# Two units ahead of the weights: reordering the start of an attention + SwiGLU kernel

## Chip, cores, metric

One core of a Trainium2 chip. The metric is device time in microseconds (us), median of several executions. A ratio in this text is the mean time of one kernel's fast runs over that of the other's fast runs of the same rounds, so it is not quite the ratio of the medians quoted beside it. In the profile's lines PE is TensorE, DVE is VectorE, ACT is ScalarE and POOL is GpSimd; square brackets give the idle time of the engine before a step and what ended it, by the profile. A profile covers one execution.

## The reference, cut

```python
B, H, S, D = 4, 8, 768, 48                # r, k, v; w, u per head and channel
for t in range(S):                        # attention with a decaying state
    cur = einsum('bhd,bhe->bhde', u * kt, vt)
    y[:, :, t] = einsum('bhd,bhde->bhe', rt, state + cur)
    state = w * state + einsum('bhd,bhe->bhde', kt, vt)
x = y.transpose(0, 2, 1, 3).reshape(3072, 384)
g = x @ w_gate                            # 384 x 1536
return (g * sigmoid(g) * (x @ w_val)) @ w_out   # 1536 x 384
```

Inputs are float64: r, k, v reach the chip as fp32, the three weights are rounded from float64 bits to fp32 inside the kernel.

## The kernel before

The sequence is cut into 24 units of 128 tokens. A unit goes through `scale` (GpSimd: khat, rhat), `turn` (TensorE transposes, ACT copies kT and rT), `diagonal` (the u term into At), `scores` (TensorE, then a masked copy on DVE), `outputs` (y, then ACT's xT) and `update` (u_ps, the state Z). Two units give a group of 12 gate/value pieces (`gv`), and later 6 projection parts (`o_ps`). Steps interleave them: step s turns unit s, scores unit s - 1, finishes unit s - 2, and in five gaps it rounds weight chunks ("R") and emits pieces ("F").

```python
def round_act():      # chunk n: magnitude and low part
    act.activation(mags[n], hi, AF.Abs, scale=2.0**-112)
    act.activation(lows[n], lo, AF.Copy, scale=2.0**-29)     # lows: two buffers
def round_dve():      # sign, then magnitude into the weight; frees the load buffer
    dve.tensor_scalar(dst, hi, -(1 << 31), None, ALU.bitwise_and)
    dve.scalar_tensor_tensor(dst, mag, 3, dst, ALU.logical_shift_left, ALU.bitwise_or)
    load_weights()
def round_pool():     # the rounding add
    pool.tensor_tensor(dst, dst, low, ALU.add)
def round_weights():  # one "R": GpSimd on chunk n, DVE on n + 1, ACT on n + 2
    if done["dve"] > done["pool"]: round_pool()
    if done["act"] > done["dve"]: round_dve()
    round_act()
def diagonal(i):
    if i < 6:
        for h in range(H): act.activation(At[i % 2][:, h, :], ident, AF.Identity, scale=du[:, h])
    else:
        pool.tensor_mul(At[i % 2], ident (broadcast), du (broadcast))
# ... cut
EARLY = [("R", "", "", "", "R"), ("R", "", "R", "", ""), ("R", "", "R", "", ""),
    ("R", "", "RF", "F", "F"), ("RF", "F", "RF", "F", "F"), ("RF", "F", "RF", "F", "RF"),
    ...]                               # the last line four times; later steps "F" only
```

A piece f of the first two groups is emitted only when its chunks (2 per pair of pieces) have had their add emitted; otherwise "F" does nothing.

Of the kernel before, what the change touches and what calls it, by code (L numbers as in the profile page):

```python
# [9 lines left out]
FP32 = mybir.dt.float32  # L10
INT32 = mybir.dt.int32
UINT32 = mybir.dt.uint32
AF = mybir.ActivationFunctionType
ALU = mybir.AluOpType
AX = mybir.AxisListType
P = 128
# [6 lines left out]
def fast(  # L23
# [25 lines left out]
    B, H, S, D = r.shape  # L49
    D2 = 2 * D  # L50
    VW = 2 * D + 16
    HP = H // 2
    NCH = S // P
    N = B * NCH
# [6 lines left out]
    ps_a = ctx.enter_context(tc.tile_pool(name="ps_a", bufs=5, space=bass.MemoryType.PSUM))  # L61
# [40 lines left out]
    def load_v(i):  # L102
        c, b = divmod(i, B)
        rows = slice(P * c, P * (c + 1))
        for e in range(2):
            sp.dma_start(
                out=v_ld[i % 4][:, :, 64 * e : 64 * e + D],
                in_=v[b, :, rows, :].rearrange("(a e) t d -> e t a d", e=2)[e],
            )
# [22 lines left out]
    def load_weights():  # L132
        n = next_chunk("load")
        if n is not None:
            src = chunks[n][0].bitcast(INT32)
            bits[n] = three.tile([P, WN, 2], INT32, name="w_bits", tag="w_bits")
            sp.dma_start(
                out=bits[n][:].rearrange("p (c f) two -> p c (f two)", c=src.shape[1]), in_=src
            )
# [5 lines left out]
    def round_act():  # L145
        n = next_chunk("act")
        if n is not None:
            lo, hi = bits[n][:, :, 0], bits[n][:, :, 1]
            mags[n] = two.tile([P, WN], INT32, name="w_mag", tag="w_mag")
            lows[n] = two.tile([P, WN], INT32, name="w_low", tag="w_low")  # L150
            act.activation(
                mags[n][:].bitcast(FP32), hi.bitcast(FP32), AF.Abs, scale=float(2.0**-112)
            )
            act.activation(lows[n][:], lo.bitcast(UINT32), AF.Copy, scale=float(2.0**-29))

    def round_dve():
        n = next_chunk("dve")
        if n is not None:
            dst = chunks[n][1].bitcast(INT32)
            c = dst.shape[1]  # L160
            hi = bits.pop(n)[:, :, 1].rearrange("p (c f) -> p c f", c=c)
            mag = mags.pop(n)[:].rearrange("p (c f) -> p c f", c=c)
# [4 lines that stand above are left out]
    def round_pool():  # L167
        n = next_chunk("pool")
        if n is not None:
            dst = chunks[n][1].bitcast(INT32)  # L170
            low = lows.pop(n)[:].rearrange("p (c f) -> p c f", c=dst.shape[1])
            pool.tensor_tensor(dst, dst, low, ALU.add)  # L172

    def round_weights():

        if done["dve"] > done["pool"]:
            round_pool()
        if done["act"] > done["dve"]:
            round_dve()
        round_act()  # L180
# [3 lines left out]
    def own_product(i):  # L184
        kl, rl = k_ld[i % 2], r_ld[i % 2]
        rk = two.tile([P, H, D], FP32, name="rk", tag="rk")
        pool.tensor_mul(rk[:], rl[:], kl[:])  # L187
        pool.tensor_mul(rk[:], rk[:], ub[:])  # L188
        du = three.tile([P, H], FP32, name="du", tag="du")
        dve.tensor_reduce(du[:], rk[:], axis=AX.X, op=ALU.add)  # L190
        dus[i] = du
# [9 lines left out]
        in_=bass.AP(tensor=u.tensor, offset=u.offset, ap=[[0, P], [1, H * D]]),  # L201
    )
    load(1)
    for n in range(3):
        load_weights()

    make_identity(nc, ident[:])

# [13 lines left out]
    for l in range(7):  # L222
        n = 1 << l
        f = sq[:, l, :].unsqueeze(2).to_broadcast([D2, HP, n])
        dve.tensor_mul(pw[:, :, P - 2 * n : P - n], pw[:, :, P - n : P], f)
    for n in (1, 0):
# [5 lines left out]
            act.copy(kscale[:].rearrange("p h d -> p (h d)"), x)  # L232
        else:
            dve.reciprocal(rscale[:].rearrange("p h d -> p (h d)"), x)
    dve.tensor_mul(
        wL[:], sq[:, 7, :].unsqueeze(2).unsqueeze(3).to_broadcast([D2, HP, 2, D]),
        own[:].unsqueeze(1).unsqueeze(3).to_broadcast([D2, HP, 2, D]),
    )

    pool.memset(mask[:], 1.0)  # L240
    pool.affine_select(
        out=mask[:], in_=mask[:], compare_op=ALU.is_gt, fill=0.0,
        base=0, pattern=[[1, P]], channel_multiplier=-1,
    )
    own_product(0)
    own_product(1)


    dve.tensor_tensor(bad[:], held[:], wcol[:], ALU.not_equal)
    dve.tensor_reduce(badc[:], bad[:], axis=AX.X, op=ALU.add)  # L250
    dve.memset(ones[:], 1.0)
    n_ps = ps_a.tile([P, HP, P], FP32, name="n_ps", tag="a")
    pe.matmul(n_ps[0:1, 0, 0:1], badc[:], ones[:], start=True, stop=True)
    act.copy(outside, n_ps[0:1, 0, 0:1])


    turned = {}

    def scale(i):
        pool.tensor_mul(khat[i % 4][:], k_ld[i % 2][:], kscale[:])  # L260
        pool.tensor_mul(rhat[i % 2][:], r_ld[i % 2][:], rscale[:])  # L261
        load_v(i)
        if i + 2 < N:
            load(i + 2)

    def diagonal(i):

        du = dus.pop(i)
        if i < 6:
            for h in range(H):  # L270
                act.activation(At[i % 2][:, h, :], ident[:], AF.Identity, scale=du[:, h : h + 1])
        else:
            pool.tensor_mul(  # L273
                At[i % 2][:], ident[:].unsqueeze(1).to_broadcast([P, H, P]),
                du[:].unsqueeze(2).to_broadcast([P, H, P]),
            )

    def pair(t, a):
        return t[:, 2 * a : 2 * a + 2, :].rearrange("p e d -> p (e d)")
# [1 line left out]
    def turn(i):  # L281
        for nm, t in (("kT", khat[i % 4]), ("rT", rhat[i % 2])):
            tp = ps_a.tile([P, HP, P], FP32, name="tp", tag="a")
            for a in range(HP):
                pe.transpose(tp[0:D2, a, :], pair(t, a), ident[:])  # L285
            if nm == "kT":
                for e in range(2):
                    act.activation(  # L288
                        kT[i % 2][:, :, e, :], tp[0:D2], AF.Identity, scale=own[:, e : e + 1]
                    )  # L290
            else:
                turned[i] = three.tile([D2, HP, P], FP32, name=nm, tag=nm)
                act.copy(turned[i][:], tp[0:D2])  # L293

    def scores(i, half):
        ps = ps_a.tile([P, HP, P], FP32, name="s_ps", tag="a")
        for n in range(4):
            a, e = divmod(4 * half + n, 2)
            pe.matmul(  # L299
                ps[:, n, :], kT[i % 2][:, a, e, :], turned[i][:, a, :],  # L300
                start=True, stop=True, skip_group_check=True,
            )
        dve.copy_predicated(  # L303
            At[i % 2][:, 4 * half : 4 * half + 4],
            mask[:].bitcast(INT32).unsqueeze(1).to_broadcast([P, HP, P]), ps[:],
        )
# [28 lines left out]
    def update(i):  # L335
# [17 lines left out]
        else:  # L353
            dve.tensor_add(z[:], ps[:], z[:])  # L354
            pool.tensor_mul(z[:], z[:], wL[:].rearrange("p a e d -> p a (e d)"))  # L355


    hT = {}

# [37 lines left out]
    def feed(n):  # L397
        for _ in range(n):
            ready = [k for k, (need, _) in enumerate(todo) if need <= done["pool"]]
            if ready:  # L400
                todo.pop(ready[0])[1]()

    def queue(g):
        parts = [(NW, lambda p=p: project(g - 1, p // 3, p % 3)) for p in range(6)] if g > 1 else []
        if g == 2:
            todo.extend((NW, lambda p=p: project(0, p // 3, p % 3)) for p in range(6))
        for f in range(FC):
            need = 2 * (f // 2) + 2 if g < 2 else NW
            todo.append((need, lambda f=f: gate_value(g, f)))
            if parts and 2 <= f < 8:  # L410
                todo.append(parts.pop(0))


    EARLY = [
        ("R", "", "", "", "R"),
        ("R", "", "R", "", ""),
        ("R", "", "R", "", ""),
        ("R", "", "RF", "F", "F"),
        ("RF", "F", "RF", "F", "F"),
        ("RF", "F", "RF", "F", "RF"),  # L420
        ("RF", "F", "RF", "F", "RF"),
        ("RF", "F", "RF", "F", "RF"),
        ("RF", "F", "RF", "F", "RF"),
    ]

    def gap(s, n):
        for what in EARLY[s][n] if s < len(EARLY) else ("F" * (3, 2, 2, 3, 2)[n]):
            if what == "R":
                round_weights()
            else:  # L430
                feed(1)

    round_weights()
    scale(0)
    for s in range(N + 2):
        if 1 <= s <= N:
            diagonal(s - 1)
        if s + 1 < N:
            if s > 0:
                own_product(s + 1)  # L440
            scale(s + 1)
        if s < N:
            turn(s)
        gap(s, 0)
        if 1 <= s <= N:
            scores(s - 1, 0)
            gap(s, 1)
            scores(s - 1, 1)
        gap(s, 2)
        if s >= 2:  # L450
            outputs(s - 2)
            if s % 2:
                queue((s - 3) // 2)
            gap(s, 3)
            update(s - 2)
        gap(s, 4)
    assert done["pool"] == NW
    feed(len(todo))
    for p in range(6):
# [414 lines left out]
```

## Time and profile before

| | kernel before |
|---|---|
| median | 737.14 us (736.28 to 738.16, 6 runs) |
| span in the profile | 736.8 us |
| TensorE busy | 696.1 us (94%) |
| first gate/value piece | 47.6 us |
| hole in TensorE | 115 to 124 us |

Two things take time here besides TensorE's own work: the first 47 us, and the hole. The lines that show both are in the prediction below. How to read them: where one engine is busy to the end, the time is its work plus what it failed to do early; so count the work done by a given moment, not the idle time of the others.

### The profile page before, as it was taken

To read this page: it belongs to the slowest core of one execution; us is meant where nothing else is said; L and a number is where in the kernel's file an instruction comes from. 1 tells how busy PE (TensorE), PEld (TensorE's weight loads), DVE (VectorE), ACT (ScalarE), POOL (GpSimd) and SP (SyncE) were. 2 spreads that over 40 slices of the span, in tenths; PEclk is the share of its full clock that TensorE was granted. 3 is DMA by queue.
4 is the path that set the end of the run, shared out by engine and by line. 5 is a ranking of instruction groups with operands and counts; after the bars stand their busy time and mean duration, and the time that the engine had idled before them with its cause. 6 is when DMAs were issued, how large, how long until landed. Compare 5 with 4: busy or idle time off the path is not lost.

```text
span 736.8 us, 10255 instructions
## 1 busy us (share of the span) xinstructions
PE 696.1 (94%) x4298; PEld 558.2 (76%) x4298; DVE 223.4 (30%) x443; ACT 165.1 (22%) x352; POOL 184.0 (25%) x159
## 2 busy tenths in 40 slices
PE   2669997999999999999999999999999999999997
PEld 2558886867788787787788787788788778777773
DVE  6755566302222132222132232222223212212120
ACT  2965652211111121111121122021111112011110
POOL 5974526430303030303033033032122211000000
PEclk9779998999999999999999999999999999999999
DMA  8974461120201010201021020111100000000000
GB/s 218 255 212 126 111 171 23 33 55 1 44 12 33 12 43 1 44 12 33 12 44 33 12 44 12 31 29 26 33 23 12 12 12 2 12 11 2 11 12 25
DMA packets 85768, 33.99 MB, mean 46 GB/s; under 512 B 76368, under 2 KB 79568, under 8 KB 85712
## 3 DMA queue, kind: packets, MB, share of 16 engines
q1 hardware_dynamic: 82256, 28.52, 16.5%
q10 hardware_dynamic: 3456, 4.72, 1.8%
q8 instruction: 36, 0.59, 0.3%
q14 instruction: 20, 0.16, 0.1%
HBM read 28.51 MB, written 4.72 MB: 45 GB/s over the span
## 4 chain that ended last, share of the span: by engine, by line
PE 88%; POOL 5%; issue 2%; DMA 1%; DVE 1%; ACT 1%; SPq 0%; POOLq 0%
PE gv L366 49%; PE o_ps L384 25%; PE y_ps L329 5%; PE s_ps L299 5%; PE tp L285 2%; PE u_ps L342 2%; DMA r_ld<-in_r_dram 1%; POOL rk L187 1%; POOL wo L172 1%; POOL wg L172 1%; POOL rhat L261 1%; POOL rk L188 1%; POOL khat L260 1%; ACT xT L333 1%; DVE wo L164 0%
## 5 line engine op out<-in xcount | busy, mean ns | idle before, releaser
L366 PE MATMUL gv<-xT,wg 128*128 128x256 f32 x864 | 215.5, 386 | 15.0 <-ACT xT L333 9.9
L366 PE MATMUL gv<-xT,wv 128*128 128x256 f32 x864 | 212.4, 382 | 0.0
L384 PE MATMUL o_ps<-wo,hT 128*128 128x384 f32 x576 | 197.0, 487 | 0.6 <-ACT o_sb L390 0.6
L366 PEld LDWEIGHTS gv<-xT,wg 128*128 128x128 f32 x864 | 159.8, 192 | 46.4 <-ACT xT L333 12.1
L373 DVE TENSOR_TENSOR sg<-sg,gv 128x256 f32<-128x256 f32 x144 | 60.5, 420 | 413.1 <-ACT sg L372 413.1
L366 PEld LDWEIGHTS gv<-xT,wv 128*128 128x128 f32 x864 | 165.9, 192 | 23.1
L384 PEld LDWEIGHTS o_ps<-wo,hT 128*128 128x128 f32 x576 | 107.8, 190 | 62.5 <-ACT o_sb L390 1.2
L372 ACT ACTIVATE sg<-gv 128x256 f32<-128x256 f32 x144 | 55.2, 384 | 402.9 <-PE gv L366 402.9
L355 POOL TENSOR_TENSOR Z<-Z,wL 96x384 f32<-96x384 f32 x16 | 16.1, 1008 | 359.4 <-DVE Z L354 359.4
L374 DVE TENSOR_TENSOR hT<-sg,gv 128x256 f32<-128x256 f32 x144 | 60.5, 420 | 4.9
L299 PEld LDWEIGHTS s_ps<-rT,kT 96*128 96x128 f32 x384 | 52.5, 204 | 6.3 <-ACT rT L293 0.3
L299 PE MATMUL s_ps<-rT,kT 96*128 96x128 f32 x384 | 52.8, 287 | 0.0
L303 DVE COPY_PREDICATED At<-mask,s_ps 128x512 f32<-128x512 int32 x48 | 34.3, 732 | 45.3 <-PE s_ps L299 45.3
L273 POOL TENSOR_TENSOR At<-ident,du 128x1024 f32<-128x1024 f32 x18 | 34.1, 1894 | 38.0 <-PE y_ps L329 38.0
L329 PE MATMUL y_ps<-At,v_ld 128*32 128x128 f32 x768 | 34.9, 273 | 0.0
L288 ACT ACTIVATE kT<-tp,own 96x512 f32<-96x512 f32 x48 | 30.1, 675 | 1.3 <-PE tp L285 0.5
L329 PE MATMUL y_ps<-rT,Z 96*32 96x128 f32 x480 | 30.2, 278 | 0.0
L329 PEld LDWEIGHTS y_ps<-At,v_ld 128*32 128x32 f32 x768 | 29.1, 109 | 0.9 <-issue 0.8
L187 POOL TENSOR_TENSOR rk<-r_ld,k_ld 128x384 f32<-128x384 f32 x24 | 27.6, 1148 | 4.3 <-DMA r_ld<-in_r_dram 4.3
L390 ACT COPY o_sb<-o_ps 128x384 f32<-128x384 f32 x24 | 11.5, 479 | 73.7 <-PE o_ps L384 73.7
L260 POOL TENSOR_TENSOR khat<-k_ld,kscale 128x384 f32<-128x384 f32 x24 | 24.0, 999 | 13.3 <-PE u_ps L342 13.3
L333 ACT COPY xT<-y_ps 128x384 f32<-128x384 f32 x24 | 11.5, 478 | 63.7 <-PE y_ps L329 63.7
(55 smaller groups left out, 341.2 us busy)
## 6 DMA issues: line engine op xcount, KB each, us to landing
k_ld<-in_k_dram SPq DMA_DIRECT2D x24, 192.0 KB, 2.8
r_ld<-in_r_dram SPq DMA_DIRECT2D x24, 192.0 KB, 3.3
w_bits<-in_moe_w_gate_dram SPq DMA_DIRECT2D x6, 768.0 KB, 6.9
w_bits<-in_moe_w_val_dram SPq DMA_DIRECT2D x6, 768.0 KB, 5.9
v_ld<-in_v_dram SPq DMA_DIRECT2D x48, 96.0 KB, 2.6
w_bits<-in_moe_w_out_dram SPq DMA_DIRECT2D x6, 768.0 KB, 4.4
out_dram<-o_sb ACTq DMA_DIRECT2D x24, 192.0 KB, 1.9
ub<-in_u_dram SPq DMA_DIRECT2D x1, 192.0 KB, 4.8
```

The costliest lines, as they stand in the source:

```text
L187: pool.tensor_mul(rk[:], rl[:], kl[:])
L260: pool.tensor_mul(khat[i % 4][:], k_ld[i % 2][:], kscale[:])
L273: pool.tensor_mul(At[i % 2][:], ident[:].unsqueeze(1).to_broadcast([P, H, P]), du[:].unsqueeze(2).to_broadcast([P, H, P]),)
L288: act.activation(kT[i % 2][:, :, e, :], tp[0:D2], AF.Identity, scale=own[:, e : e + 1])
L299: pe.matmul(ps[:, n, :], kT[i % 2][:, a, e, :], turned[i][:, a, :], start=True, stop=True, skip_group_check=True,)
L303: dve.copy_predicated(At[i % 2][:, 4 * half : 4 * half + 4], mask[:].bitcast(INT32).unsqueeze(1).to_broadcast([P, HP, P]), ps[:],)
L329: pe.matmul(ps[32 * q : 32 * q + 32, cc, :], *rows[q][n], start=(n == 0), stop=(n == len(rows[q]) - 1), skip_group_check=True,)
L366: pe.matmul(gv[:, o, :].rearrange("p (i t) -> p i t", i=2), wt[:, c, P * f : P * (f + 1)], xT[:, 2 * g % NX : 2 * g % NX + 2, c, :], start ...
L372: act.activation(sg[:], gv[:, 0, :], AF.Sigmoid)
L373: dve.tensor_mul(sg[:], sg[:], gv[:, 0, :])
L374: dve.tensor_mul(hT[g][:, f, :], sg[:], gv[:, 1, :])
L384: pe.matmul(ps[:], hT[g][:, f, P * j : P * (j + 1)], wo[:, f, :], start=(f == 0), stop=(f == FC - 1),)
```

## The change

The intent: get TensorE to its first pieces early, by sending units 0 and 1 through turn, scores and y back to back with only two of 18 weight chunks rounded, then give it six pieces a step in steps 6 to 9. In passing, the diagonals of the first six units go from ACT to GpSimd.

```diff
-    for n in range(3):
-        load_weights()
+    load_weights()
+    load_v(0)
+    load_weights()
+    load_v(1)
+    load_weights()
 # ... in diagonal(i):
-        if i < 6:
-            for h in range(H):
-                act.activation(At[i % 2][:, h, :], ident[:], AF.Identity, scale=du[:, h : h + 1])
-        else:
-            pool.tensor_mul(...)
+        pool.tensor_mul(...)
 # ... the count of decay values out of range moves from the start to step 12
+    EARLY = {3: ("RF", "F", "RF", "", "F"), 4: ("RF", "F", "RF", "F", "RF"),
+        5: ("RF", "F", "RF", "F", "RF"), 6: ("RF", "F", "RFF", "F", "RF"),
+        7, 8, 9: as 6}
+    scale(0); scale(1)
+    round_act(); round_act(); round_dve()
+    turn(0); turn(1)
+    diagonal(0); scores(0, 0); scores(0, 1); diagonal(1)
+    round_pool(); round_dve()
+    scores(1, 0); scores(1, 1)
+    round_pool(); own_product(2); scale(2); round_act()
+    outputs(0); outputs(1); queue(0)
+    own_product(3); scale(3)
+    # ... wL
+    turn(2); feed(1); update(0); round_weights(); feed(1); update(1)
-    for s in range(N + 2):
+    for s in range(3, N + 2):
```

More of the change, by code (lines that the diff above doesn't have):

```diff
@@ L234, in fast @@
             dve.reciprocal(rscale[:].rearrange("p h d -> p (h d)"), x)
-    dve.tensor_mul(
-        wL[:], sq[:, 7, :].unsqueeze(2).unsqueeze(3).to_broadcast([D2, HP, 2, D]),
-        own[:].unsqueeze(1).unsqueeze(3).to_broadcast([D2, HP, 2, D]),
-    )
+    own_product(0)
+    own_product(1)
     pool.memset(mask[:], 1.0)
@@ L244, in fast @@
     )
-    own_product(0)
-    own_product(1)
-    dve.tensor_tensor(bad[:], held[:], wcol[:], ALU.not_equal)
-    dve.tensor_reduce(badc[:], bad[:], axis=AX.X, op=ALU.add)
-    dve.memset(ones[:], 1.0)
-    n_ps = ps_a.tile([P, HP, P], FP32, name="n_ps", tag="a")
-    pe.matmul(n_ps[0:1, 0, 0:1], badc[:], ones[:], start=True, stop=True)
-    act.copy(outside, n_ps[0:1, 0, 0:1])
     turned = {}
@@ L261, in scale @@
         pool.tensor_mul(rhat[i % 2][:], r_ld[i % 2][:], rscale[:])
-        load_v(i)
+        if i >= 2:
+            load_v(i)
         if i + 2 < N:
@@ L268, in diagonal @@
         du = dus.pop(i)
-        if i < 6:
-            for h in range(H):
-                act.activation(At[i % 2][:, h, :], ident[:], AF.Identity, scale=du[:, h : h + 1])
-        else:
-            pool.tensor_mul(
-                At[i % 2][:], ident[:].unsqueeze(1).to_broadcast([P, H, P]),
-                du[:].unsqueeze(2).to_broadcast([P, H, P]),
-            )
+        pool.tensor_mul(
+            At[i % 2][:], ident[:].unsqueeze(1).to_broadcast([P, H, P]),
+            du[:].unsqueeze(2).to_broadcast([P, H, P]),
+        )
     def pair(t, a):
@@ L355, in update, with count_outside @@
             pool.tensor_mul(z[:], z[:], wL[:].rearrange("p a e d -> p a (e d)"))
+    def count_outside():
+        dve.tensor_tensor(bad[:], held[:], wcol[:], ALU.not_equal)
+        dve.tensor_reduce(badc[:], bad[:], axis=AX.X, op=ALU.add)
+        dve.memset(ones[:], 1.0)
+        n_ps = ps_a.tile([P, HP, P], FP32, name="n_ps", tag="a")
+        pe.matmul(n_ps[0:1, 0, 0:1], badc[:], ones[:], start=True, stop=True)
+        act.copy(outside, n_ps[0:1, 0, 0:1])
     hT = {}
@@ L411, in queue, with gaps @@
                 todo.append(parts.pop(0))
-    EARLY = [
-        ("R", "", "", "", "R"),
-        ("R", "", "R", "", ""),
-        ("R", "", "R", "", ""),
-        ("R", "", "RF", "F", "F"),
-        ("RF", "F", "RF", "F", "F"),
-        ("RF", "F", "RF", "F", "RF"),
-        ("RF", "F", "RF", "F", "RF"),
-        ("RF", "F", "RF", "F", "RF"),
-        ("RF", "F", "RF", "F", "RF"),
-    ]
-    def gap(s, n):
-        for what in EARLY[s][n] if s < len(EARLY) else ("F" * (3, 2, 2, 3, 2)[n]):
+    def gaps(s, n):
+        for what in EARLY[s][n] if s in EARLY else ("F" * (3, 2, 2, 3, 2)[n]):
             if what == "R":
@@ L431, in gap @@
                 feed(1)
+    EARLY = {
+        3: ("RF", "F", "RF", "", "F"),
+        4: ("RF", "F", "RF", "F", "RF"),
+        5: ("RF", "F", "RF", "F", "RF"),
+        6: ("RF", "F", "RFF", "F", "RF"),
+        7: ("RF", "F", "RFF", "F", "RF"),
+        8: ("RF", "F", "RFF", "F", "RF"),
+        9: ("RF", "F", "RFF", "F", "RF"),
+    }
+    scale(0)
+    scale(1)
+    round_act()
+    round_act()
+    round_dve()
+    turn(0)
+    turn(1)
+    diagonal(0)
+    scores(0, 0)
+    scores(0, 1)
+    diagonal(1)
+    round_pool()
+    round_dve()
+    scores(1, 0)
+    scores(1, 1)
+    round_pool()
+    own_product(2)
+    scale(2)
+    round_act()
+    outputs(0)
+    outputs(1)
+    queue(0)
+    own_product(3)
+    scale(3)
+    dve.tensor_mul(
+        wL[:], sq[:, 7, :].unsqueeze(2).unsqueeze(3).to_broadcast([D2, HP, 2, D]),
+        own[:].unsqueeze(1).unsqueeze(3).to_broadcast([D2, HP, 2, D]),
+    )
+    turn(2)
+    feed(1)
+    update(0)
     round_weights()
-    scale(0)
-    for s in range(N + 2):
-        if 1 <= s <= N:
+    feed(1)
+    update(1)
+    for s in range(3, N + 2):
+        if s <= N:
             diagonal(s - 1)
         if s + 1 < N:
-            if s > 0:
-                own_product(s + 1)
+            own_product(s + 1)
             scale(s + 1)
@@ L443, in fast @@
             turn(s)
-        gap(s, 0)
-        if 1 <= s <= N:
+        gaps(s, 0)
+        if s <= N:
             scores(s - 1, 0)
-            gap(s, 1)
+            gaps(s, 1)
             scores(s - 1, 1)
-        gap(s, 2)
-        if s >= 2:
+        gaps(s, 2)
+        if s >= 4:
             outputs(s - 2)
@@ L453, in fast @@
                 queue((s - 3) // 2)
-            gap(s, 3)
+            gaps(s, 3)
             update(s - 2)
-        gap(s, 4)
+        gaps(s, 4)
+        if s == 12:
+            count_outside()
     assert done["pool"] == NW
```

## The prediction

> **What bounds the kernel now.** I read the page's 40 slices first, then TensorE's waits, then the chain of waits, then the engines' timelines of the first 140 us.
>
> The slices say that TensorE (PE) is the bound from about 55 us on, and is not before that:
>
> ```profile
> PE   2669997999999999999999999999999999999997
> POOL 5974526430303030303033033032122211000000
> PEclk9779998999999999999999999999999999999999
> ```
>
> One slice is 18.4 us. The first three PE digits are 2, 6, 6, the seventh is 7, and all others are 9 but the last. The granted clock dips in the second, third and seventh slices. So there are two losses: the start, and a hole near 120 us. TensorE's waits before 130 us give them names (total, times, longest):
>
> ```profile
> PE t_ps L229 <- DVE pw L225: 7.9, 1, 7.9
> PE gv L366 <- ACT xT L333: 6.4, 2, 5.8
> PE n_ps L253 <- DVE ones L251: 5.5, 1, 5.5
> PE gv L366 <- DVE hT L374: 5.1, 2, 4.2
> PE u_ps L342 <- DVE At L303: 3.4, 1, 3.4
> ```
>
> After 130 us only 4.2 us of waits are left in 607 us. From there on the time is TensorE's work, so a gain can only come from having done more of it by some early moment. The chain of waits gives the price list of that work, and shows the hole (start, us, what):
>
> ```profile
> 44.43 1.82 POOL wg L172
> 46.28 0.91 ACT w_low L154
> 47.19 0.37 ACT xT L333
> 47.60 5.49 PE gv L366 x12
> ...
> 60.23 0.89 PE s_ps L299 x8
> 61.13 2.59 PE gv L366 x12
> ...
> 67.20 1.03 PE y_ps L329 x32
> ...
> 71.03 0.68 PE u_ps L342 x8
> ...
> 74.32 0.87 PE tp L285 x8
> ...
> 112.35 1.85 POOL At L273
> ...
> 119.19 2.48 POOL wo L172
> ```
>
> At full clock a gate/value piece (gv) costs 2.6, a turn of one unit (tp) 0.87, both halves of its scores 2 x 0.89 = 1.8, a first-chunk y 1.03, an update (u) 0.68. The first piece starts at 47.60 and at half clock (5.49 with one update inside, not 2.6): before it, xT waited on ACT behind weight rounding (w_low), and that on GpSimd's (POOL) rounding adds.
>
> A ledger makes the start one number. Done before 47.6: 4 tp (3.5) + 3 scores (5.4) + 2 y (2.1) + 1 u (0.7) = 11.6 us at full clock. From 47.6 to 54 the clock is 0.50 to 0.56, so 6.4 us hold 3.3 of work. At 54 us TensorE has 14.9 us behind it: it is **39.1 us in arrears**, and then keeps pace.
>
> The hole at 115.1 to 123.9 (0.83 + 4.25 us idle) is one chain: an update's result goes to DVE, to GpSimd's Z (1.24), a rounding add, the diagonal (1.85), rk, rk, khat, rhat, another add; ACT's w_low waits for that, and the sigmoid stands behind w_low. After it the clock is 0.5 for some 5 us, worth 2.5.
>
> **What the Trainium skill says.** "TensorE: Matmul & The Clock Gate", What's actually happening: the array falls to half clock after an idle window of about 3.4 us and comes back after a busy one. The trace agrees: the half-clock stretches here last 6.8 us (23.0 to 29.8, 33.3 to 40.1, 46.9 to 53.8), each after about 3.4 us in which TensorE was at most 45% busy. Same page, Architectural detail: ACT and DVE queues are strict first-in first-out. The trace agrees: the sigmoid that fills the hole starts at 122.50, right behind the w_low it does not need. "SBUF — State Buffer", Who interferes with whom: a DVE instruction with two SBUF inputs contends with GpSimd reads. The trace agrees: DVE's magnitude step (two inputs) takes 0.96 alone and 2.07 beside GpSimd, 5.26 at worst; GpSimd's adds take 1.8 and up to 2.55, rk 1.0 and up to 1.79.
>
> **The change part by part.** The order of instructions on each engine was read from both builds.
>
> (a) Prologue: weight chunk 0, v0, chunk 1, v1, chunk 2 are loaded in this order; then units 0 and 1 are scaled, turned, scored and multiplied out with only chunks 0 and 1 rounded. Work on TensorE is unchanged.
>
> (b) The diagonals of units 0 to 5 go from ACT (8 activations, 2.43 each set) to GpSimd (1.89 each): ACT loses 14.6 us, GpSimd gains 11.3, nearly all inside the stretch in which GpSimd feeds TensorE its weights.
>
> (c) Six pieces instead of five per step in steps 6 to 9; in steps 3 to 5 a piece is emitted only when its weight pair is rounded. The instruction order shows that in step 3 only two pieces go out, in step 4 two, both after GpSimd adds.
>
> (d) The small matmul that counts decay values goes late: its 5.5 us wait overlapped the wait for khat anyway, so nothing by itself.
>
> Walk through the start with the durations of before:
> - Chunk 1 landed at 13.8. It now sits behind v0 (192 B runs; such loads landed at about 185 GB/s, 0.2 MB = 1.1): 15.0.
> - ACT w_mag, w_low of chunk 1 (1.7) 16.7, kT 1.2, rT 0.5: 18.4. Scores of unit 0: 20.2. DVE's masked copy to 20.9, chunk 1's two steps 1.9: 22.8. GpSimd add of chunk 1 (2.0): 24.8. GpSimd rk, rk, khat, rhat of unit 2, 4.3 (4.0 alone, 4.7 crowded): 29.1. TensorE turns unit 2 and starts **the first piece at 29.7** instead of 47.6.
> - Then GpSimd decides: unit 3 (4.3) 33.4, diagonal 1.9 35.3, unit 4 39.6, add 1.8 41.4, add 2.2: 43.6. TensorE by then has only 2 pieces, 2 u, tp, scores = 9.3 us to do, over by 42.4 even with one half-clock stretch (+3.4). It waits for the third piece's weights until 43.6.
> - TensorE: rest of that piece 1.3, next 2.6, tp 0.9, scores 1.8: 50.2. GpSimd: diagonal 45.5, unit 5 49.8, adds 51.6 and 53.8. TensorE waits again, then 1.3, y 1.0 (56.1), piece 58.7, u 59.4, tp 60.3, half a piece 61.6.
> - GpSimd: add 55.6, diagonal of unit 4 after that y (56.1) 58.0, rk twice 60.4, khat after that u, rhat 62.3, add 2.2: **64.5**. TensorE waits 2.9 us; later waits close up, since a step with six pieces is about 17 to 20 us of TensorE against 11 of GpSimd.
>
> Ledger at 64.5: 6 tp 5.2 + 4 scores 7.2 + 3 y 3.1 + 3 u 2.0 + 6.5 pieces 16.9 = 34.4; arrears 30.1. **Gain 39.1 - 30.1 = 9.0 us**, half of the 17.9 by which the first piece moves.
>
> Against it: the 2.9 us wait probably costs a half-clock stretch. A full one takes 3.4; I put 60% on it: 2.0. The hole of step 7 stays: the same chain of Z, add, diagonal, four products, add stands ahead of the same sigmoid, and the extra piece comes behind it. Its short part (0.83) now comes in two steps instead of one: 0.8. Sum: 736.7 - 9.0 + 2.0 + 0.8 = **730.5 us**.
>
> **Rivals.** (1) TensorE stays fed from the first piece on: arrears at 29.7 would be about 29.7 - 11 = 19, gain 20, 717 us. For it: DMA and ACT have room. Against: each pair of pieces needs two adds, and GpSimd's order puts 4.3 + 1.9 + 4.3 us of unit work ahead of them. (2) GpSimd and DVE get in each other's way more than assumed: with rk 1.7, adds 2.5 and DVE steps of 2 us, the 64.5 becomes 66 to 67, always with a half-clock stretch: gain 4, 733; with another hole in step 6 (where by my walk the sigmoid is ready only 0.2 us before TensorE wants it) 737. (3) The hole of step 7 closes because ACT has no diagonals and the queue has more pieces: another 7.6 us, 723. Against: ACT waited there for GpSimd, not for its own work. (4) Chunk 1 or v lands late: one to one after the first 1.2 us, since GpSimd idles that long before chunk 1's add.
>
> **Range and chances.** The walk has some twenty hand-overs and an unknown clock phase: 722.5 to 737.5. Over 2% faster needs 722.0, a gain of 14.7, that is rival 1 or 3: 0.09. Over 2% slower needs a new long wait in the dense part: 0.02.
>
> **What would show it.** First piece at about 30 us. TensorE waits of some 1 to 4 us for GpSimd's wg/wv adds, near 40, 51 and 62, and none of note between 66 and 100. Half clock near 26 to 33 and after the last of these waits. The hole of about 5 us ended by hT remains, around 105 to 112. GpSimd near 100% busy from 10 to 60 us. It is wrong if the waits at 40 to 65 name DMA or ACT, if the first piece starts after 35, or if the hole is gone.

## The result

737.26 us (736.64 to 737.74, 6 runs) against 737.14: ratio 1.0001, 95% interval 0.9988 to 1.0014. **The same.** A gain of 6.2 us had been forecast; the time lies inside the stated range, at its very end.

The slices of the page after the change:

```profile
PE   3877997999999999999999999999999999999996
POOL 6897634733030303030303033032032211000000
PEclk9999998999999999999999999999999999999999
```

The first three TensorE digits went from 2, 6, 6 to 3, 8, 7, but the fourth fell from 9 to 7: work was done earlier and idle time moved later. GpSimd's third and fourth digits rose from 7 and 4 to 9 and 7. Its load in the same stretch, from the changed kernel's first unit-2 product to its last early wait (stretch, length, then busy time of TensorE, weight loads, DVE, ACT, GpSimd; clock; DMA share; GB/s), first in the kernel before, then in the changed one:

```profile
27.34:69.50 42.16, 32.95 (x240) 29.01 (x239) 25.67 (x34) 28.11 (x57) 28.92 (x21) 0.81 0.71 187
```

```profile
27.34:69.50 42.16, 30.59 (x207) 25.50 (x198) 29.00 (x39) 22.50 (x34) 38.15 (x30) 0.96 0.68 175
```

ACT lost 5.6 us of work there, GpSimd gained 9.2 and is 90% busy. TensorE's waits before 130 us after the change (engine, line waited for, total, times, longest):

```profile
PE tp L272 <- POOL khat L250: 7.5, 3, 4.1
PE gv L362 <- POOL wv L172: 6.0, 3, 3.6
PE gv L362 <- DVE hT L370: 5.5, 3, 4.2
PE gv L362 <- POOL wg L172: 2.5, 2, 1.5
```

The long waits for xT (5.8) and At (3.4) are gone, 0.6 us for xT stays; waits for GpSimd's adds (wv, wg) have come. The hole ended by hT is there as before. The chain of waits of the changed kernel shows what set the pace (start, us, what):

```profile
9.15 6.39 DMA w_bits<-in_moe_w_val_dram
...
18.92 3.80 PE s_ps L286 x16
22.74 0.73 DVE At L290
...
24.41 0.97 DVE wv L164
...
25.52 1.82 POOL wv L172
...
31.96 4.29 PE gv L362 x12
...
46.66 4.17 PE gv L362 x18
...
53.51 2.21 DVE wv L164
...
57.92 0.97 DVE wg L164
...
59.37 1.05 POOL wg L172
...
61.14 1.90 POOL At L260
...
67.69 1.81 POOL wv L172
...
69.55 2.92 PE gv L362 x6
```

From chunk 1's landing through ACT, the first scores, DVE and GpSimd to the first piece at 31.8 us. From there to 69.50 the chain spends about 15 us on GpSimd (the adds between 41 and 47, then everything from 59.37 on), 12 on DVE (36.7 to 41.0 and 51.3 to 58.9) and 8.5 on TensorE's own pieces, up to the add that lets TensorE go on at 69.55. So GpSimd is not alone on it.

The ledger again. At 69.55 us TensorE had the same 34.4 us of work behind it that the prediction counts for 64.5. It is 35.15 us in arrears; the kernel before stands at 39.1. That leaves **3.9 us**. The half clock after the 3.58 us wait takes 1.7 (half a piece and half the scores took 3.87 from 69.55 to 73.42 instead of 2.19), a wait in step 6 takes 0.4, the second short wait for hT (140 us) 0.8. What remains is 1.0, and the span of the profiled run is 735.8 against 736.8. The ledger is no better than about 1 us, though: it leaves out 0.6 us less waiting for xT after 130 us (3.0 against 3.6) and 0.4 less for the first piece after the hole (4.91 against 5.27). Over the timed runs even that is not clear of noise.

### The profile page after: what moved, and what is told of

The parts are those of the page before. It is cut to its first block, busy times and chain, and to the rows that moved or that the text cites. A ratio compares the mean times of both kernels' runs of the same rounds, so it can differ in the third digit from the quotient of the medians.

```text
span 735.8 us, 10203 instructions
## 1 busy us (share of the span) xinstructions
PE 695.3 (95%) x4298; PEld 555.3 (75%) x4298; DVE 228.8 (31%) x443; ACT 152.0 (21%) x304; POOL 195.5 (27%) x165
## 4 chain that ended last, share of the span: by engine, by line
PE 85%; POOL 5%; DVE 4%; issue 3%; ACT 1%; SPq 1%; DMA 1%; POOLq 0%; DVEq 0%; ACTq 0%
PE gv L362 47%; PE o_ps L380 25%; PE s_ps L286 5%; PE y_ps L316 4%; PE tp L272 2%; PE u_ps L329 1%; POOL wv L172 1%; DMA w_bits<-in_moe_w_val_dram 1%; DVE wo L164 1%; POOL rhat L251 1%; POOL wo L172 1%; POOL khat L250 1%; POOL At L260 1%; POOL wg L172 1%; POOL rk L187 0%
## 5 line engine op out<-in xcount | busy, mean ns | idle before, releaser
L260 POOL TENSOR_TENSOR At<-ident,du 128x1024 f32<-128x1024 f32 x24 | 45.4, 1893 | 38.0 <-PE y_ps L316 38.0
L187 POOL TENSOR_TENSOR rk<-r_ld,k_ld 128x384 f32<-128x384 f32 x24 | 26.0, 1084 | 4.5 <-DMA r_ld<-in_r_dram 4.5
L251 POOL TENSOR_TENSOR rhat<-r_ld,rscale 128x384 f32<-128x384 f32 x24 | 25.6, 1066 | 0.0
```

Of the source, the lines that this page charges most:

```text
L251: pool.tensor_mul(rhat[i % 2][:], r_ld[i % 2][:], rscale[:])
L260: pool.tensor_mul(At[i % 2][:], ident[:].unsqueeze(1).to_broadcast([P, H, P]), du[:].unsqueeze(2).to_broadcast([P, H, P]),)
```

## The experiments

Differences against the changed kernel are worked out from ratios: (1.0001 - ratio) x 737 us. Each run shares its chip with runs of the kernel before.

**1. Diagonals back on ACT.**

```diff
 def diagonal(i):
-    pool.tensor_mul(...)
+    if i < 6: eight act.activation(...)      # as in the kernel before
+    else: pool.tensor_mul(...)
```

> The changed kernel with the diagonals of units 0 to 5 back on ACT (8 activations each), as in the kernel before. Theory A (GpSimd's own work is what TensorE waits for between 40 and 70 us): the three diagonals on that path, 1.9 us each, go; the last wait for an add of wv ends at 64 to 66 us instead of 69.5, and the time falls by 3.5 to 5.5 us, to about 732.5. Theory B (the adds wait for DVE's rounding steps and for DMA, GpSimd only looks busy): the wait still ends at 68 or later, time within 1.5 us of the changed kernel.

732.72 us, ratio 0.9943 (0.9927 to 0.9959): 4.3 us less than the changed kernel. TensorE's waits at the three adds, which stood at 46.66, 57.74 and 69.55, now end here:

```profile
45.36 1.56 PE L366 MATMUL gv<-xT,wv 128*128 128x256 f32 x6 [1.71 <-POOL wv L172]
55.19 1.56 PE L366 MATMUL gv<-xT,wv 128*128 128x256 f32 x6 [1.72 <-POOL wv L172]
66.25 1.56 PE L366 MATMUL gv<-xT,wv 128*128 128x256 f32 x6 [2.82 <-POOL wv L172]
```

The last restart comes 3.3 us earlier (0.6 of it may be the load's: ACT's step on chunk 1 began at 14.98 in this execution, at 15.56 in the changed kernel's), and no half clock follows it (1.56, not 2.92, for half a piece). Theory A holds: the time is within the expected 3.5 to 5.5 us, the wait ends 0.25 us after the expected 64 to 66. Three products of 1.9 us were taken away and no more than 3.3 us came back at this wait. DVE is still ahead of the last add: its step for wv ends at 64.24, and the add begins at 64.37.

**2. Three diagonals twice on GpSimd.**

```diff
-        pool.tensor_mul(At..., ident..., du...)
+        for _ in range(2 if 2 <= i < 5 else 1):
+            pool.tensor_mul(At..., ident..., du...)
```

> The changed kernel with the diagonal product of units 2, 3 and 4 done twice on GpSimd (same result, 3 x 1.87 us more). Theory A: the last wait for wv moves from 69.5 to 73 to 75 us and the time grows by 3.5 to 5.5 us. Theory B: under 1.5 us.

742.72 us, ratio 1.0089 (1.0072 to 1.0107): 6.5 us more for 5.6 us of work. The last wait ends at 74.76, 5.2 us later:

```profile
74.76 2.93 PE L363 MATMUL gv<-xT,wv 128*128 128x256 f32 x6 [5.55 <-POOL wv L172]
```

From there on the two profiles run in parallel, and the spans differ by 5.0 us. The mean over the timed runs is further off because two of the six executions took 745 us, the other four 742.5 to 742.9. The first wait is also longer (3.86 us, up to 45.77) and half clock follows it, but that lies ahead of the last wait, which swallows it. So work added to GpSimd in this stretch is on the path nearly in full; taken away (run 1), it comes back only in part.

**3. Only the diagonals, in the kernel before.**

```diff
 def diagonal(i):          # kernel before
-    if i < 6:
+    if i < 0:
```

> The kernel before with only part (b) of the change: the diagonals of units 0 to 5 on GpSimd instead of ACT. In its first 47 us GpSimd is already 90 to 100% busy and hands the weights on. If theory A is right, the products of the units ahead of the first piece, 1.9 us each for units 0, 1 and 2, delay it and the time grows by 4 to 7 us, about the size of what the changed kernel gains without them (4.2 us). If part (b) costs only in the new order: under 1.5 us.

743.31 us, ratio 1.0077 (1.0063 to 1.0091): 5.7 us more than the kernel before. Its chain of waits ahead of the first piece has the products in it:

```profile
29.78 2.57 POOL At L273
...
40.57 2.58 POOL At L273
...
49.54 1.83 POOL wg L172
51.39 0.91 ACT w_low L154
52.30 0.38 ACT xT L333
52.72 5.30 PE gv L366 x12
```

The first piece starts at 52.72 instead of 47.60. Together with 1 this splits the change: the reordering with its new piece counts is worth 0.9943 alone, the move of the diagonals costs 1.0077 in the old order (4.3 us in the new one), and together they come to nothing clear of noise.

**4. The first scores at half clock: idle transposes.**

```diff
+    idle_ps = ps_o.tile([P, DM], FP32, ...)      # never read
+    18 pe.transpose(idle_ps[:, 0:P], ident, ident) before own_product(0), 2 after turn(0), 4 after turn(1)
```

> The changed kernel with 24 idle transposes on TensorE between 9 and 19 us (into a PSUM bank that nothing reads), so that the first scores find TensorE busy. Theory C (the first scores ran at half clock although the record shows none, 3.80 us for what takes 1.8, and that delay runs through DVE, GpSimd's add of chunk 1 and everything after): scores of units 0 and 1 take 3.6 us together instead of 6.7, the first piece starts 1.5 to 2.3 us earlier (29.5 to 30.3), the time falls by 1 to 2.5 us. Rival: the first scores are slow for another reason (PSUM, weight loads), nothing moves.

736.62 us, ratio 0.9986 (0.9967 to 1.0005). **Inconclusive for the time.** The array did warm up (four transposes took 0.64 us instead of 1.09), and the scores of both units took 5.47 us instead of 6.73:

```profile
17.39 0.60 PE L242 MATMUL idle_ps<-ident 128*128 128x128 f32 x4
19.89 5.47 PE L293 MATMUL s_ps<-rT,kT 96*128 96x128 f32 x32 [1.90 <-ACT rT L287]
```

But chunk 1 landed 1.0 us later in this run (ACT's step on it began at 16.52, not 15.56), and the 1.90 us of idle time ahead of the scores were followed by half clock from 21.2 on. The first piece started at 31.71, as in the changed kernel (31.80). Counted from ACT's step on chunk 1 it came after 15.2 us instead of 16.2: in this one profile the faster scores did reach the path, and the late load took the gain back.

**5. v behind the weight chunks.**

```diff
-    load_weights(); load_v(0); load_weights(); load_v(1); load_weights()
+    for n in range(3): load_weights()
+    load_v(0); load_v(1)
```

> The changed kernel with v of units 0 and 1 loaded behind the third weight chunk instead of between the chunks. Chunk 1 then lands about 1.1 us earlier (14.4 instead of 15.5 us), ACT's steps and the first scores start 1.1 us earlier. If the load is first on the path, as the chain of waits has it, the first piece starts about 1 us earlier and the time falls by up to 1 us; if v then comes too late for the first y (at 25.6 us), the gain is lost there.

734.82 us, ratio 0.9972 (0.9954 to 0.9991): 2.1 us less, twice what was expected. ACT's step on chunk 1 began at 13.99 (15.56 in the changed kernel), the add of chunk 1 on GpSimd at 23.97 instead of 25.51. The first piece started 1.5 us earlier (30.26), and the last wait ended 1.1 earlier (68.44). So the load of chunk 1 is first on the path, as the chain has it, and v can wait. The interval reaches nearly to no gain, and one execution's landing is a rough measure: ACT's step on chunk 1 began between 14.41 and 16.52 in the seven profiles that have the changed kernel's load order, between 13.58 and 13.99 in the four with v behind. The direction is shown, the size is rough.

**6. A third buffer for w_low, in both kernels.**

```diff
-    lows[n] = two.tile([P, WN], INT32, name="w_low", tag="w_low")
+    lows[n] = three.tile([P, WN], INT32, name="w_low", tag="w_low")
```

> The changed kernel with three buffers instead of two for the rounded low part (w_low). Theory D (the hole at 111 to 124 us is the sigmoid standing behind w_low on ACT, and w_low waits only because its buffer is still read by GpSimd's late add): the waits of 0.83 and 4.23 us ended by hT and the half clock after them are gone, also the 0.83 at 140; the time falls by 6 to 9 us, to about 729. Rival: the next add is late as well, DVE's masked copies and rounding wait behind it, or the pieces after it need that chunk: a hole of 2 us or more stays and the gain is under 4 us.

> The same one line in the kernel before. Theory D: its hole (0.83 + 4.25 us and some 2.5 us of half clock at 115 to 129 us) goes, the time falls by 5 to 8 us, to about 730. Then changed kernel and kernel before again differ by no more than 2 us. Rival: under 4 us.

Changed kernel: 731.51 us, ratio 0.9927 (0.9910 to 0.9944), 5.5 us less. Kernel before: 730.52 us, ratio 0.9917 (0.9901 to 0.9932), 6.1 us less. TensorE's waits for hT in the changed kernel with the third buffer (1.27 is now the longest, 4.23 before):

```profile
PE gv L362 <- DVE hT L370: 2.9, 3, 1.3
```

Theory D holds for the long wait, and its half clock went with it. The size is a little under the lower end for the changed kernel because short waits of 0.83 and 1.27 us stay. The long wait shrank alike in both kernels (from 4.23 and 4.25 to 1.27): the hole has nothing to do with the change, and the change did not touch it. That the whole gain is about the same in both is partly chance: in the kernel before, the third buffer also let the first piece start at 45.26 instead of 47.60.

**7. One piece less in steps 6 to 9.**

```diff
-        6: ("RF", "F", "RFF", "F", "RF"),   # and 7, 8, 9
+        6: ("RF", "F", "RF", "F", "RF"),
```

> The changed kernel with one piece less in steps 6 to 9 (as many as the kernel before has in its last early steps). Theory: from 70 us on TensorE is dense but for the hole, so that it does not matter which work it has: within 1.5 us of the changed kernel. Rival: the extra piece widens TensorE's lead over GpSimd's adds, so that the hole is shallower with it: 2 us or more slower without it.

741.24 us, ratio 1.0060 (1.0044 to 1.0076): 4.3 us slower. **The expectation was wrong**, the rival as well in its reason: the hole of step 7 is as deep as ever (4.23). Two waits come later than it, after 140 us:

```profile
PE n_ps L350 <- DVE ones L348: 2.1, 1, 2.1
PE gv L362 <- DVE hT L370: 1.2, 1, 1.2
```

With fewer pieces done early, step 8 still has pieces where the changed kernel has projections. A piece needs ACT and DVE for its hT; a projection needs no DVE, and ACT only for the copy at its end. So a piece waits for hT in step 8, and the small counting matmul of step 12 waits 2.1 us, because a piece stands right before it and DVE makes that piece's product (until 279.4) before it counts (`ones` at 280.04). These two waits, 3.3 us, are most of the 3.8 us by which the spans differ. That it does not matter which work a dense TensorE has did not hold. The run takes a piece from step 9 too, where the kernel before has twelve, so it is not that kernel's schedule.

**8. Everything that helped, then DVE further ahead.** First, the combination with idle transposes; then with the load order of 5; then both.

```diff
 # combo:      diagonals on ACT + three w_low buffers + idle transposes
 # best:       diagonals on ACT + three w_low buffers + v behind the chunks
 # best_warm:  best + idle transposes
 # ahead:      best, with four w_low buffers and
     feed(1)
     update(1)
+    round_dve()
+    round_act()
     for s in range(3, N + 2):
```

> The changed kernel with the diagonals of units 0 to 5 on ACT, three w_low buffers and the idle transposes. If theories A, C and D hold together: 4 + 1.5 + 7.5 us, 13 us less, about 724 us (1.8% less than the kernel before). If the gains hide one another (ACT becomes the bound with its diagonals back, or the clock), 728 or more.

> The changed kernel with diagonals of units 0 to 5 on ACT, three w_low buffers and v behind the third weight chunk. The three gains measured alone (4.3, 5.4 and 2.1 us against the changed kernel) add up to 11.8, about 725; against the combination with idle transposes (726.7) it tells what the load order is worth beside them. If the load order is hidden once GpSimd is relieved: 727 or more.

> The same with the 24 idle transposes. Theory C (first scores at half clock, on the path): 1 to 2 us less than without them. If the first scores are hidden behind ACT's diagonal activations by now (the masked copy waited for those in the run with ACT diagonals): within 0.7 us.

> As the one before the last, with DVE and ACT rounding one chunk further ahead of GpSimd (four w_low buffers, one extra DVE step and ACT step ahead of step 3). Theory E (the adds of wv in steps 3 to 5 wait for DVE's two-input step, which is held off by the GpSimd add before it; 1 to 1.7 us each time): TensorE's three waits for wv between 40 and 66 us, 6.0 us together in the combination, shrink to 3 or less and the time falls by 1.5 to 3 us to about 722.5. If GpSimd's own order is the limit even then: within 1 us.

| kernel | median | ratio to the kernel before (95%) |
|---|---|---|
| combo | 726.67 us | 0.9876 (0.9858 to 0.9894) |
| best | 726.44 us | 0.9847 (0.9834 to 0.9859) |
| best_warm | 726.96 us | 0.9856 (0.9839 to 0.9873) |
| ahead | 722.47 us | 0.9801 (0.9788 to 0.9813) |

combo missed its expectation: 9.2 us less than the changed kernel, not 13, between the theories' 724 and the rival's 728. best: the gains measured alone add up (11.8 expected, 11.4 found). Idle transposes give nothing on top: the scores of both units fell from 5.07 to 3.74 us, but the masked copy waits for ACT's diagonals and started no earlier (20.07 against 19.79), as the rival said. Combo ran in other rounds than the last three, so its distance from best is only what two ratios tell: 0.3%.

ahead: 3.4 us less than best (0.9801 against 0.9847). TensorE's waits for wv in best, then in ahead:

```profile
PE gv L365 <- POOL wv L172: 5.8, 3, 2.8
```

```profile
PE gv L366 <- POOL wv L173: 3.1, 3, 1.7
```

Theory E holds in size: the total falls by 2.7 us, wg's by 0.4. At TensorE this is 1.6 us at the last restart (62.18 against 63.77) and 1.7 us of half clock that follows this restart in best's profile and not in ahead's. Why DVE was late can be read in the changed kernel's timeline of DVE (start, us): its two-input step for wv begins at 42.83, while GpSimd's wg add runs from 42.01 to 43.83, and lasts 1.81 instead of 0.96; GpSimd's next add, for wv, starts when it ends.

```profile
42.83 1.81 DVE L164 SCALAR_TENSOR_TENSOR wv<-w_mag,wv 128x768 int32<-128x768 int32 x1
```

The view puts that add's wait down to ACT's w_low, which ended at 44.79:

```profile
44.78 1.82 POOL L172 TENSOR_TENSOR wv<-wv,w_low 128x768 int32<-128x768 int32 x1 [0.96 <-ACT w_low L154]
```

The code says otherwise. With GpSimd on chunk n, DVE is on n + 1 and ACT on n + 2: this add is chunk 3's, and so is DVE's step, which ended at 44.64. The w_low that ended at 44.79 is chunk 4's, and the add does not read it; chunk 3's was ready at 38.3. So this add waited for DVE. That ahead gains by this alone is not shown, since it moves ACT's step and adds a buffer as well.

**ahead beats both kernels**: 722.47 us, 2.0% less than the kernel before (1.9 to 2.1), correct.

## Why the prediction was wrong

Point by point, by its own steps.

- *What bounds, and the ledger*: right for the start. The gain there is what TensorE has done by the moment it runs without waits; the first piece moved by 15.8 us, and of that 3.9 were left at the restart, not the 9.0 of the forecast. (Later, the order of the work counts too: run 7.)
- *The walk*: its order is right, **the step that failed is the size of the time up to "64.5"**, the end of the last add that TensorE waits for. It was 69.5. Where the 5.0 us arose, by the walk's own marks:
  - First scores: "20.2" and the masked copy "20.9" were 22.7 and 23.5; the add of chunk 1 ended at 27.3, not 24.8. That is 2.5 us. I had priced the first scores at full clock (1.8); they took 3.80. The kernel before had shown it: its first transposes took 1.06 us, later ones 0.60, and its first scores 2.59. Chunk 1 being 0.5 us late is the smaller part. That the slow scores cost time was not shown alone (4 is inconclusive for the time); that everything after them moves with chunk 1 is (5).
  - The adds in pairs: wv's add ended at 46.6 and 57.7, not 43.6 and 53.8. The lag grows from 2.4 us at the add of chunk 2 (wg, ended at 43.8) to 3.9. I gave the pair's second add 2.2 us; it took 1.8 after a gap of 1.0, in which it waited for DVE's two-input step on its chunk (see 8).
  - The next wg add: I let it start at once at 53.8. It waited 1.7 us for DVE and ended at 61.2, not 55.6 (5.6 us behind). 0.6 came back in the units' products, hence 5.0 at the end.
- *Part (b)*: I wrote that GpSimd takes on 11.3 us "nearly all inside the stretch in which GpSimd feeds TensorE its weights", put 1.9 per product into the walk, and stopped there. So its cost was inside the forecast and is not what made it wrong; but it was never weighed against part (a) as a cost of its own. Runs 1 and 3 do: 4.3 and 5.7 us, about all that the reordering gains.
- *Rival 2* came nearest: GpSimd and DVE in each other's way. Its size was too small as well: "66 to 67" for the 64.5, against 69.5. Its 737 needed another hole in step 6, where the wait was 0.4, so that this number fits is luck. Its reason was half right: single products and DVE steps did reach 1.72 and 2.42 us, but the adds took 1.8, with gaps between them while DVE catches up.
- *The half clock* after the last wait: estimated at 2.0, measured 1.7. *The hole and its second short part*: right (4.23 us; 0.8). *Step 6*: the margin of 0.2 us was in fact a wait of 0.4.
- *Part (c)* was misread for step 9, which goes from twelve pieces or projection parts to six, and was taken to be without effect on the dense part. Run 7 says that one piece more in steps 6 to 9 is worth 4.3 us, mostly because TensorE then has projections where a piece would wait for DVE. So the gain of "reordering" in run 1 includes them.
- *Part (d)*: no cost in the changed kernel; in run 7 its new place costs 2.1 us.
- *Chances*: 0.89 on "within 2%" was right. The forecast gain of 6.2 us was not there: 5.0 of it went in the walk and 0.4 in step 6; the rest is within the ledger's 1 us.

## What to carry to other kernels

When a stage is moved forward, ask what feeds it next and follow that engine to the moment at which nobody waits any more: here the first piece came 16 us earlier, but only 4 us of it were left when the last wait for the rounding engines, GpSimd and DVE, had ended, and later small losses took most of those. Do not load the feeding engine in the same change: the six products moved to GpSimd cost as much as the reordering won. And measure the parts of a change that comes out even; two effects of 4 to 6 us may be cancelling, and the hole beside them may be one buffer deep.

## What the Trainium skill lacked or had wrong

- "TensorE: Matmul & The Clock Gate", What's actually happening, has the array throttled by default until activity releases it. The runs agree, and I missed it: the first scores (16 records) took 3.80 us, the same 16 records 1.95 us at 40.9. What the page lacks is that the clock row of a profile shows 1.00 up to its first recorded change, so that a cold start is invisible there.
- The same section has half clock return after an idle window of about 3.4 us. In the run with idle transposes 1.90 us without work (17.99 to 19.89) were followed by half clock from 21.2 on; in the kernel before a stretch of 3.4 us that was 43% busy (19.6 to 23.0) was followed by it. A partly idle window can do. Of four profiles with a wait of 2.8 us at the last add, two (best, best_warm) have half clock after it and two (act_diag, combo) do not, so whether such a wait costs more than itself differs from run to run.
- "SBUF — State Buffer", Who interferes with whom: its contention rule for a DVE instruction with two SBUF inputs (an exclusive lock) agrees with the 1.81 us step above (0.96 alone; it ended 0.8 us after GpSimd's add). It lacks what follows when that step feeds the next GpSimd instruction: each then waits for the other in turn, here a gap of 0.96 us in GpSimd in two pairs of adds (44.78, 55.86).
- No page that I used says that a wait which a profile puts down to one engine can belong to another that ended within 0.15 us of it: the wv add at 44.78 stands under ACT's w_low (end 44.79), which is another chunk's, while DVE's step on its own chunk ended at 44.64.
